# Half a feed-forward piece carried across a step boundary, with Softplus and Erf at later places

## The chip, the cores and the metric

The kernel runs on one core of a Trainium2 chip. The metric is the time of one execution in microseconds (us), as the device measures it. The engines are named as in the profile: PE is the matrix engine, PEld its weight loads, DVE the vector engine, ACT the scalar (activation) engine, POOL the third elementwise engine, and SP the engine that only issues DMAs. A small q behind a name (ACTq, SPq) means the engine's instruction queue, where DMAs are issued.

## The reference

Two blocks follow each other. The first is a linear attention with a decaying state, over 4 sequences of 768 tokens, 8 heads of width 48:

```
for t in range(S):
    cur = einsum('bhd,bhe->bhde', u * kt, vt)
    y[:, :, t] = einsum('bhd,bhde->bhe', rt, state + cur)
    state = wt[..., None] * state + einsum('bhd,bhe->bhde', kt, vt)
```

Its result, as x of 3072 tokens by 384, goes through a feed-forward block with 2048 hidden columns:

```
h = x @ w_in
sp = maximum(h, 0) + log1p(exp(-abs(h)))      # softplus
g = h * erf(sp)
out = g @ w_out
```

All of it is in 32-bit floating point.

## The kernel before

The tokens are cut into 12 steps (`s` from 0 to 11) of 256 tokens: two sequences, 128 tokens each. In step `s`, `attend` (line 350) computes the attention of these tokens. It runs through six levels of masked products (line 390 on PE, into a PSUM tile `pp`), then transposes and state products, and ends with the products at line 498 that finish `y` in PSUM. ACT copies `y` out (lines 505 to 508), and small DMAs issued from SP and ACT (line 512) put the remaining rows into place, so that the tile `xT` holds x, transposed.

The feed-forward of step `s` comes later and is spread in pieces between the attention work of the following steps. It has two generators:

- `hidden` (line 520) makes h = x @ w_in. It works in 8 pieces for a step. A piece is six matmul calls (two column blocks, `ff` 0 and 1, of three accumulating matmuls each), which the trace shows as 12 records at line 547, because each 32-bit matmul stands in it as two. They fill a PSUM tile `m`, which one ACT copy (line 554) moves to the tile `h` in SBUF. Four pieces make one half of the hidden columns. After the last piece of a half, `activate` puts three stages into the list `later`: Softplus (ACT, line 529), Erf (ACT, line 532) and the multiplication (DVE, line 536), each over the whole half.
- `project` (line 559) makes out = g @ w_out.

The PSUM pool of the tiles `m` has two buffers. A third piece can therefore write only when the copy of the one two places before it has been made.

Each step calls `place` eight times: after each of the six levels (places 0 to 5), after the transposes (place 6) and after the state products (place 7). What a place puts into the engines' queues is written out by hand, and each engine takes it in that order. In steps 1 and 2, listed in the table `ALONE`, a place does this, in this order: `convert_at` (the weights are converted there: DVE lines 196 and 199, POOL line 203, then ACT lines 187 and 189 for the next pair of blocks, then a load), `advance(ALONE[s][n])` (takes that many stages from `later`; 0 takes none), and `beside`, which takes one piece of `hidden` of step s - 1:

```
            if s in ALONE:
                convert_at(n)
                advance(ALONE[s][n])
            ...
            beside(s, next(places))
```

So the 8 pieces of step 0's hidden columns lie at the 8 places of step 1, and those of step 1 at the places of step 2. The first piece in step 2 needs `xT` of step 1, which has only just been made at the end of step 1. Where PE would wait for it, `stay_warm` (line 373) puts matmuls of 512 columns whose result nobody reads: one in step 1, two in step 2.

While the weights are converted (to the start of step 3), all the products of `attend` use one of the two `pp` buffers, since the conversion uses the other. The first level's products of step 2 thus need the last reader of the buffer in step 1, the state's update on DVE (line 484), to be done.

Of the kernel before, what the change touches and what calls it, by code (L numbers as in the profile page):

```python
# [22 lines left out]
FG = 8  # L23
FT = 2
# [23 lines left out]
def rights(ap, half):  # L48

    names = "abcdefg"[: len(ap.shape) - 1]  # L50
    spread = " ".join(names)
    return ap.rearrange(f"{spread} (n two h) -> {spread} n two h", two=2, h=half)[
        (slice(None),) * len(names) + (slice(None), 1)
    ]
# [3 lines left out]
def kernel(  # L58
# [25 lines left out]
    NG = NT // FG  # L84
# [37 lines left out]
    def products(shape):  # L122


        n = 0 if turns["converting"] else turns["next"]
        turns["next"] = 1 - n
        return ps_p.tile(shape, FP32, name=f"pp{n}")
# [89 lines left out]
    def rows(e, n=D):  # L217
        return slice(e * EP, e * EP + n)
# [7 lines left out]
    def scale(s, level):  # L226

        in_t, tots = loaded[s][0], ready[s][1]
        half, nb = 1 << (level - 1), JP * C >> level
        halves = view(in_t[:, 0:2], half, [[JP * C - half, 2], [2 * half, nb], [1, half]])  # L230
        nc.vector.tensor_mul(  # L231
            halves, halves, view(tots[level - 1], 0, [[1, 2], [2, nb], [0, half]])
        )
# [116 lines left out]
    def attend(s, xT, place, behind):  # L350
# [14 lines left out]
        def keep_busy(*columns):  # L365
            zeros = states[1][0][:].rearrange("p n d -> p (n d)")
            for n in columns if not s else ():
                nc.tensor.matmul(
                    y[:].rearrange("p e j q t -> p (e j q t)")[:, :n], lhsT=ident[:],
                    rhs=zeros[:, :n], start=True, stop=True, skip_group_check=True,  # L370
                )

        def stay_warm(times=1):
            for _ in range(times):
                ps = ps_m.tile([P, NP * C], FP32, name="m")
                nc.tensor.matmul(
                    ps[:], lhsT=ident[:], rhs=in_t[:, 2, :NP], start=True, stop=True
                )

        for level in range(NEAR_LOG + 1 if s >= DIRECT else 1, LOG + 1):  # L380
            half = 1 << (level - 1)
            rk = made[:] if level == 1 else RK

            pp = products([P, NE, JP, HC])
            m = HC if level <= MASKED else half
            for n in range(JP):
                for s0 in range(0, C, HC):
                    for e in range(NE):
                        t0 = s0 if level <= MASKED else s0 + half
                        nc.tensor.matmul(  # L390
                            pp[s0 : s0 + m, e, n, :m],
                            lhsT=rk[rows(e), 1, n, s0 : s0 + m],
                            rhs=rk[rows(e), 0, n, t0 : t0 + m],
                            start=True,
                            stop=True,
                        )
            keep_busy(DM, DM // 2)
            if level == 1 and s in ALONE:
                stay_warm(s)
            scale(s, level)  # L400
            got = pp[:].rearrange("p e n t -> p (e n) t")
            if level == 1:
                if not s:
                    nc.vector.tensor_copy(out=first[:], in_=mask_sb[:, 0, :])
                nc.vector.tensor_mul(
                    own[:], got, first[:, None, :].to_broadcast([P, NH, HC])
                )
            elif level <= MASKED:
                nc.vector.copy_predicated(  # L409
                    rights(own[:], half),  # L410
                    rights(mask_sb[:, level - 1 : level, :].to_broadcast([P, NH, HC]), half),
                    rights(got, half),
                )
            else:
                for s0 in range(0, C, HC):
                    nc.scalar.copy(  # L416
                        own[s0 : s0 + half, :, half:], got[s0 : s0 + half, :, :half]
                    )
            if level > (NEAR_LOG if s >= DIRECT - 1 else 1):
                next(following, None)  # L420
            place(level - 1)
# [95 lines left out]

    later = []

    def hidden(xT, gs):  # L520


        def activate(h):

            held = []

            def softplus():
                held.append(act.tile([P, FG, UNIT], FP32, name="sp"))
                nc.scalar.activation(held[0][:], h[:], AF.Softplus)  # L529

            def erf():
                nc.scalar.activation(held[0][:], held[0][:], AF.Erf)  # L532

            def multiply():
                for part in (slice(0, FG // 2), slice(FG // 2, FG)):
                    nc.vector.tensor_mul(h[:, part], h[:, part], held[0][:, part])  # L536

            later.extend([(softplus, True), (erf, True), (multiply, False)])

        for g in range(NG):  # L540
            h = hid.tile([P, FG, UNIT], FP32, name="h")
            gs.append(h)
            for f in range(0, FG, FT):
                ps = ps_m.tile([P, FT, UNIT], FP32, name="m")
                for ff in range(FT):
                    for kk in range(KT):
                        nc.tensor.matmul(  # L547
                            ps[:, ff, :],
                            lhsT=w_in_sb[:, g * FG + f + ff, kk * P : (kk + 1) * P],
                            rhs=xT[:, kk, :],  # L550
                            start=kk == 0,
                            stop=kk == KT - 1,
                        )
                nc.scalar.copy(h[:, f : f + FT, :], ps[:])  # L554
                if f == FG - FT:
                    activate(h)
                yield

    def project(s, gs):

        c, i = divmod(s, SPC)
        ps = [None] * NJ
        for g in range(NG):
            for j in range(NJ):
                if not g:
                    ps[j] = ps_m.tile([P, DM], FP32, name="m")
                for f in range(FG):
                    nc.tensor.matmul(  # L568
                        ps[j][:],
                        lhsT=gs[g][:, f, j * C : (j + 1) * C],  # L570
                        rhs=w_out_sb[:, g * FG + f, :],
                        start=g + f == 0,
                        stop=g == NG - 1 and f == FG - 1,
                    )
                    if g == NG - 1 and f == FG - 1:
                        o = outs.tile([P, DM], FP32, name="o")
                        nc.scalar.copy(o[:], ps[j][:])  # L577
                        nc.sync.dma_start(out=out[i * NJ + j, c], in_=o[:])
                    if f % 4 == 3:
                        yield  # L580

    xTs, hids, projs = {}, {}, {}
    gated = [[] for _ in range(n_steps)]

    def advance(count=None):

        while later and count != 0:
            stage, last = later.pop(0)
            stage()
            count = count and count - 1  # L590
            if last and not count:
                break

    def beside(s, k):


        kind, of, pieces = (projs, s - 3, 2) if k < 4 else (hids, s - 1, 2)
        if s >= DIRECT:
            kind, of = (projs, s - 3) if k < 2 else (hids, s - 1)
            pieces = (4, 4, 3, 3, 2)[k]  # L600
        if s in ALONE:
            kind, of, pieces = hids, s - 1, 1
        if not 0 <= of < n_steps:
            return
        if of not in kind:
            kind[of] = hidden(xTs[of], gated[of]) if kind is hids else project(of, gated[of])
        for _ in range(pieces):
            next(kind[of])

# [5 lines left out]
        ("js", "j"),  # L615
    )

    ALONE = {1: (0, 0, 0, 0, 0, 0, 1, 0), 2: (1, 0, 0, 0, 0, 0, 1, 1)}

    make_identity(nc, ident[:])  # L620
    nc.vector.memset(y[:], 0.0)
# [3 lines left out]
    with tc.manual_schedule(  # L625
# [19 lines left out]
        for s in range(n_steps):  # L645
# [3 lines left out]
            def convert_at(n):  # L649
                if s < len(CONVERT) and n < len(CONVERT[s]):  # L650
                    for what in CONVERT[s][n]:
                        conversion.send(what)

            def place(n):
# [3 lines that stand above are left out]
                else:  # L658
                    advance()
                    convert_at(n)  # L660
                beside(s, next(places))
# [6 lines left out]
        for k in range(15):  # L668
            advance()
            beside(n_steps + k // 5, k % 5)  # L670
# [97 lines left out]
```

## Time and profile before

| what | value |
|---|---|
| time, median of 3 runs | 637.16 us (637.15 to 637.78) |
| the profiled run: its time, its span in the profile | 637.19 us, 635.4 us |
| PE busy | 622.5 us (98%), 7338 matmul records |
| ACT busy | 301.3 us (47%), 374 instructions |
| DVE busy | 306.9 us (48%), 311 instructions |
| POOL busy | 276.1 us (43%), 240 instructions |
| step 1's first hidden piece to step 2's first | 36.61 to 73.09 us |
| step 2's first hidden piece to step 3's first projection | 73.09 to 106.73 us |

A row of the timeline gives the start in us from the span's beginning, the duration in us, the engine, the line, the operation with its tiles and their shapes, and how many instructions were merged into the row. In square brackets stand the idle time of that engine just before and what ended it. Neighbouring instructions overlap a little, so the duration of a row may be longer than the distance to the next. In the chain of waits a row gives start, duration and what work the end of the program hung on in that time; "issue" is time in which nothing that the profile shows was waited for.

### The profile page before, as it was taken

The numbers are of one execution on the slowest core, as the hardware profiler recorded it, in microseconds if no ns is written. First come the engines' busy times: TensorE is split into PE (matmuls) and PEld (weight loads), VectorE is DVE, ScalarE is ACT, GpSimd is POOL, SyncE is SP. The second block draws the span as 40 slices with busy tenths as digits, with TensorE's granted clock in tenths as the row PEclk, the third lists the DMA queues.
The fourth block names the chain that finished last, engine by engine and source line by source line (L and its number), as shares of the span: only waits on it lengthen the run. The fifth ranks groups of instructions, "written<-read, shape, count | busy, mean of one in ns | idle before, by whom it ended". The sixth has DMA issues, their size and how long they took to land.

```text
span 635.4 us, 16193 instructions
## 1 busy us (share of the span) xinstructions
PE 622.5 (98%) x7338; PEld 458.2 (72%) x7338; DVE 306.9 (48%) x311; ACT 301.3 (47%) x374; POOL 276.1 (43%) x240
## 2 busy tenths in 40 slices
PE   8889999999999999999999999999999999999997
PEld 7567787678678678668668668768768758768654
DVE  4588597577346256266265365366446322011110
ACT  2537778756424544544534524624624625634520
POOL 4338175495194196097097087088079100000000
PEclk9999999999999999999999999999999999999999
DMA  8366371400500500500510410420330000000000
GB/s 326 130 241 201 136 260 56 200 15 10 206 26 10 207 26 9 206 26 10 183 49 10 168 65 9 152 81 9 103 128 11 8 13 14 7 23 3 1 25 25
DMA packets 24628, 53.84 MB, mean 85 GB/s; under 512 B 11376, under 2 KB 16752, under 8 KB 23152
## 3 DMA queue, kind: packets, MB, share of 16 engines
q1 hardware_dynamic: 23408, 52.23, 23.1%
q8 instruction: 57, 0.93, 0.6%
q10 hardware_dynamic: 1152, 0.59, 0.4%
q14 instruction: 11, 0.09, 0.1%
HBM read 46.39 MB, written 5.24 MB: 81 GB/s over the span
## 4 chain that ended last, share of the span: by engine, by line
PE 91%; DVE 3%; ACT 3%; issue 1%; DMA 1%; POOL 0%; SPq 0%; DVEq 0%; ACTq 0%
PE m L568 40%; PE m L547 38%; PE pp L390 6%; PE y L435 2%; PE pp L446 2%; PE y L498 2%; PE pp L464 2%; DVE in L231 1%; DMA in<-in_rkw 1%; ACT rk L260 1%; DVE own L409 1%; ACT own L416 0%; ACT rest L189 0%; ACT pp L187 0%; DMA xT<-y 0%
## 5 line engine op out<-in xcount | busy, mean ns | idle before, releaser
L547 PE MATMUL m<-xT,w_in_sb 128*128 128x256 f32 x1152 | 260.1, 382 | 0.6 <-DMA xT<-y 0.3
L568 PE MATMUL m<-w_out_sb,h 128*128 128x384 f32 x768 | 253.5, 489 | 0.0
L547 PEld LDWEIGHTS m<-xT,w_in_sb 128*128 128x128 f32 x1152 | 214.6, 190 | 33.2 <-issue 1.6
L568 PEld LDWEIGHTS m<-w_out_sb,h 128*128 128x128 f32 x768 | 144.2, 190 | 97.4
L231 DVE TENSOR_TENSOR in<-in,tot_sb 128x1024 f32<-128x1024 f32 x60 | 80.8, 1347 | 154.4 <-PE pp L390 153.2
L536 DVE TENSOR_TENSOR h<-h,sp 128x1024 f32<-128x1024 f32 x48 | 80.3, 1713 | 67.7 <-ACT sp L532 67.7
L554 ACT COPY h<-m 128x512 f32<-128x512 f32 x96 | 56.2, 586 | 104.2 <-PE m L547 104.0
L577 ACT COPY o<-m 128x384 f32<-128x384 f32 x24 | 11.5, 479 | 148.4 <-PE m L568 136.6
L289 POOL TENSOR_TENSOR rk<-words,u_row 128x768 f32<-128x768 f32 x8 | 17.3, 2157 | 124.8 <-DMA words<-in_rk_rows 124.8
L306 POOL TENSOR_TENSOR tot_sb<-tot_sb 128x256 f32<-128x256 f32 (+4 forms) x60 | 54.1, 902 | 4.5
L390 PEld LDWEIGHTS pp<-in 48*64 48x64 f32 (+1 forms) x2816 | 41.0, 127 | 20.5 <-issue 17.5
L295 POOL TENSOR_TENSOR words<-words,rest 128x576 f32<-128x576 f32 (+5 forms) x48 | 52.6, 1096 | 3.8
L390 PE MATMUL pp<-in 48*64 48x64 f32 (+1 forms) x2816 | 46.5, 214 | 4.2 <-DVE own L409 2.3
L532 ACT ACTIVATE sp<-sp 128x2048 f32<-128x2048 f32 x24 | 45.9, 1911 | 0.3
L529 ACT ACTIVATE sp<-h 128x2048 f32<-128x2048 f32 x24 | 45.9, 1911 | 0.3
L532 ACT ACT_TABLE_LOAD x24 | 30.8, 1283 | 20.4 <-issue 20.2
L296 POOL TENSOR_TENSOR words<-words 128x480 f32<-128x480 f32 (+4 forms) x40 | 32.8, 819 | 3.1
L529 ACT ACT_TABLE_LOAD x24 | 30.8, 1283 | 3.0 <-issue 2.6
L296 POOL TENSOR_TENSOR rk<-words 128x672 f32<-128x672 f32 (+1 forms) x16 | 31.9, 1994 | 0.6
L324 DVE TENSOR_REDUCE sums<-words 128x10 f32<-128x480 f32 (+4 forms) x40 | 17.7, 452 | 26.5 <-POOL words L296 25.9
L203 POOL TENSOR_TENSOR w_out_sb<-w_out_sb,rest 128x768 int32<-128x768 int32 x8 | 18.1, 2271 | 27.4 <-DVE w_out_sb L199 27.4
L476 DVE TENSOR_TENSOR middle<-faded,pp 48x384 f32<-48x384 f32 x20 | 11.0, 552 | 32.9 <-PE pp L464 32.6
(57 smaller groups left out, 427.2 us busy)
## 6 DMA issues: line engine op xcount, KB each, us to landing
in<-in_rkw SPq DMA_DIRECT2D x11, 1536.0 KB, 6.6
words<-in_moe_w_in SPq DMA_DIRECT2D x8, 768.0 KB, 6.0
words<-in_moe_w_out SPq DMA_DIRECT2D x8, 768.0 KB, 4.8
words<-in_rk_rows SPq DMA_DIRECT2D x8, 768.0 KB, 8.4
v<-in_v SPq DMA_DIRECT2D x12, 384.0 KB, 7.0
out<-o SPq DMA_DIRECT2D x24, 192.0 KB, 1.9
rest<-in_w_rows SPq DMA_DIRECT2D x8, 384.0 KB, 8.9
in<-in_rkw SPq DMA_DIRECT2D x2, 512.0 KB, 4.6
```

The costliest lines, as they stand in the source:

```text
L203: nc.gpsimd.tensor_tensor(out=into, in0=into, in1=rest[:], op=ALU.add)
L231: nc.vector.tensor_mul(halves, halves, view(tots[level - 1], 0, [[1, 2], [2, nb], [0, half]]))
L295: nc.gpsimd.tensor_mul(k[:, : NEAR - n], k[:, : NEAR - n], w[:, n - 1 : NEAR - 1])
L296: nc.gpsimd.tensor_mul(terms[n], r[:, n:], k[:, : NEAR - n])
L306: nc.gpsimd.tensor_mul(new, pair[:, :, 0], pair[:, :, 1])
L390: nc.tensor.matmul(pp[s0 : s0 + m, e, n, :m], lhsT=rk[rows(e), 1, n, s0 : s0 + m], rhs=rk[rows(e), 0, n, t0 : t0 + m], start=True, stop=True,)
L529: nc.scalar.activation(held[0][:], h[:], AF.Softplus)
L532: nc.scalar.activation(held[0][:], held[0][:], AF.Erf)
L536: nc.vector.tensor_mul(h[:, part], h[:, part], held[0][:, part])
L547: nc.tensor.matmul(ps[:, ff, :], lhsT=w_in_sb[:, g * FG + f + ff, kk * P : (kk + 1) * P], rhs=xT[:, kk, :], start=kk == 0, stop=kk == KT - 1,)
L554: nc.scalar.copy(h[:, f : f + FT, :], ps[:])
L568: nc.tensor.matmul(ps[j][:], lhsT=gs[g][:, f, j * C : (j + 1) * C], rhs=w_out_sb[:, g * FG + f, :], start=g + f == 0, stop=g == NG - 1 and ...
```

## The change

`hidden` is told by `cut` whether it is step 0's. If it is, the last of its eight pieces stops once more after its first column block, that is in the middle of the piece. The eighth place of step 1 then does only this first half. The first place of step 2 takes the second half, before the first piece of step 1's hidden columns; the ACT copy of the whole piece comes with the second half, and so does the entry of the second half's stages into `later`.

The two `stay_warm` matmuls at the first level of step 2 are gone; step 1 keeps its one.

`ALONE` changes as well. Softplus of step 0's first half, which stood at place 6 of step 1, is now at place 0 of step 2. Its Erf, which stood at place 0 of step 2, is now at place 2. Its multiplication stays at place 6 of step 2, and Softplus of the second half at place 7.

```diff
@@ attend
-            if level == 1 and s in ALONE:
-                stay_warm(s)
+            if level == 1 and s == 1:
+                stay_warm()
@@ hidden
-    def hidden(xT, gs):
+    def hidden(xT, gs, cut):
...
                             start=kk == 0,
                             stop=kk == KT - 1,
                         )
+                    if cut and not ff and g == NG - 1 and f == FG - FT:
+                        yield
                 nc.scalar.copy(h[:, f : f + FT, :], ps[:])
@@ beside
         if s in ALONE:
             kind, of, pieces = hids, s - 1, 1
+            if s == 2 and not k:
+
+                next(hids[0])
...
-            kind[of] = hidden(xTs[of], gated[of]) if kind is hids else project(of, gated[of])
+            kind[of] = hidden(xTs[of], gated[of], not of) if kind is hids else project(of, gated[of])
@@
-    ALONE = {1: (0, 0, 0, 0, 0, 0, 1, 0), 2: (1, 0, 0, 0, 0, 0, 1, 1)}
+    ALONE = {1: (0,) * 8, 2: (1, 0, 1, 0, 0, 0, 1, 1)}
```

## The prediction, made before the changed kernel was run

> **What bounds the kernel now.** I read the page first. Its busy line and the head of its chain say where a change can count at all.
>
> ```profile
> PE 622.5 (98%) x7338; PEld 458.2 (72%) x7338; DVE 306.9 (48%) x311; ACT 301.3 (47%) x374; POOL 276.1 (43%) x240
> PE 91%; DVE 3%; ACT 3%; issue 1%; DMA 1%; POOL 0%; SPq 0%; DVEq 0%; ACTq 0%
> ```
>
> PE is the bound. The list of PE's waits from 107 us to the end is empty, so whatever PE loses or gains before 107 us is carried to the end whole. The question is only what happens between the end of step 1 and the start of step 3. For that I took PE's timeline (from the eighth piece of step 0's hidden columns on), and then ACT's for the same stretch.
>
> ```profile
> 66.48 2.86 PE L547 MATMUL m<-xT,w_in_sb 128*128 128x256 f32 x12
> 69.27 0.66 PE L498 MATMUL y<-in,middle 48*48 48x64 f32 x32
> 69.76 1.11 PE L390 MATMUL pp<-rk 48*64 48x64 f32 x64
> 70.80 1.99 PE L376 MATMUL m<-in,ident 128*128 128x512 f32 x4
> 73.09 3.25 PE L547 MATMUL m<-xT,w_in_sb 128*128 128x256 f32 x12 [0.30 <-DMA xT<-y]
> 76.27 1.16 PE L390 MATMUL pp<-in 48*64 48x64 f32 x64
> 77.36 2.86 PE L547 MATMUL m<-xT,w_in_sb 128*128 128x256 f32 x12
> 80.38 1.16 PE L390 MATMUL pp<-in 48*64 48x64 f32 x64 [0.16 <-DVE own L409]
> ```
>
> From y's end (about 69.95) to the arrival of x at 73.09 PE has 1.04 us of needed products, 1.99 of `stay_warm` and 0.30 idle. So there is about 2.1 us to fill. I call the pieces of step 2 q0 (73.09), q1 (77.36), q2 and so on, and the moved piece p8 (66.48).
>
> ```profile
> 65.46 1.28 ACT L529 ACT_TABLE_LOAD   x1
> 66.76 1.91 ACT L529 ACTIVATE sp<-h 128x2048 f32<-128x2048 f32 x1
> 68.58 0.57 ACT L554 COPY h<-m 128x512 f32<-128x512 f32 x1
> 69.38 0.59 ACT L554 COPY h<-m 128x512 f32<-128x512 f32 x1 [0.24 <-PE m L547]
> ...
> 75.99 0.88 ACT L187 ACTIVATE pp<-words 128x768 f32<-128x768 f32 x1 [1.20 <-DVE w_out_sb L199]
> 76.81 0.91 ACT L189 ACTIVATE rest<-words 128x768 int32<-128x768 uint32 x1
> 77.73 1.28 ACT L532 ACT_TABLE_LOAD   x1
> 79.03 1.91 ACT L532 ACTIVATE sp<-sp 128x2048 f32<-128x2048 f32 x1
> 80.84 0.57 ACT L554 COPY h<-m 128x512 f32<-128x512 f32 x1
> ```
>
> The last row is what I rest on most. It is q0's copy; q0's matmuls ended at 76.34, yet the copy starts at 80.84, because Erf stands before it in ACT's queue. It ends at 81.41, and q2, which needs the buffer, starts at 81.47. It costs PE almost nothing today only because q1's buffer is free: the last user of it was a `stay_warm` matmul, which nobody reads.
>
> **What the Trainium skill says.** "PSUM — Partial Sum Buffer", section "Engine vs sequencer instructions": the queues of ScalarE, VectorE and GpSimdE are strict first in, first out. The trace agrees, by the 4.5 us of that copy. "ScalarE: Activation LUTs", section "What ACT_TABLE_LOAD costs": 1283 ns for the load, and with a drain 2.66 us for a switch. The trace has the 1283, but the function begins 1.30 us after its load, so I use 3.11 us for Erf or Softplus with its load (77.73 to 80.84). "TensorE: Matmul & The Clock Gate", section "What's actually happening": an idle window of about 3.4 us may put PE at half clock until it has been busy as long. PE's longest wait in this trace is 1.7 us, so no run shows it yet; that PE starts slow it does show (the warm-up matmuls of line 630, 128 columns, median 421 ns, fastest 275).
>
> **The change part by part.** First what gains. The first half of p8 is 6 of 12 records, half of 2.79 us, so 1.40. It ends at 66.55 + 1.40 = 67.95. The y products also need `middle`, which DVE ends at 67.31, so they run at once, end at 68.59 instead of 69.98, and everything down to the landing of x comes 1.39 us earlier: first rows at 71.70. PE meanwhile wants level 1's products. Their buffer is read by the state update on DVE (line 484), which ends at 69.38 and doesn't move. So PE idles 0.8 us, does the products from 69.42 to 70.46, and p8's second half to 71.86. The first rows of x are there. q0 has its later rows no sooner than 1.39 us earlier than now, so it ends at 76.34 - 1.39 = 74.95. This is the whole gain: 1.39 us. The 1.99 us of `stay_warm` that are gone are not counted again, since they stood in the same wait.
>
> Softplus of the first half leaves place 6 of step 1 (3.2 us of ACT). Nobody waited for it: the y copies start at 70.00, as soon as y is there. So nothing is gained. No DMA, no SP and no POOL instruction is among what moves; the weight loads on SP and the joins on POOL keep their order and are only pulled or pushed along with ACT's conversion. The number of table loads stays.
>
> Now what is queued behind it. At place 0 of step 2 ACT gets, in order: the two conversion instructions, Softplus (instead of Erf), **the copy of p8**, the copy of q0. And q1 at place 1 needs a PSUM buffer out of two: one holds p8, the other q0, and both copies stand behind Softplus. The conversion pair starts when DVE has joined the one before, which follows from the y copies: 75.99 - 1.39 = 74.60. Softplus' load then starts at 77.73 - 1.39 = 76.34, the copy of p8 at + 3.11 = 79.45, and ends at 80.02. q1 starts at about 80.06. It would have been ready at 74.95 + 1.09 (level 2's products) = 76.0. So PE waits some 4.0 us. Against before (77.40) q1 is 2.66 late. Level 3's products, which waited 0.16 for DVE (that is over by then), follow at 82.85 instead of 80.38: 2.47 late.
>
> Then Erf at place 2. It stands behind the conversion pair there and before q2's copy. Before, that pair began 5.35 us after level 3's products (80.38 to 85.73, DVE's chain of four instructions between). DVE is half a microsecond less behind then, so I take 4.85: 87.70. The pair takes 1.65, Erf 3.11, q2's copy 0.57: 93.03. q4 needs that buffer. PE gets to it at 82.85 + 3 x 1.09 + 2 x 2.79 = 91.70, so it waits 1.35. ACT is now the chain itself: next level multiplications for step 3 (1.76), a pair (1.63), q3's copy; q5 waits another 0.35 for that one. The next pair can't begin before DVE has joined the one before, at 94.68 + 0.86 + 0.04 + 0.97 + 0.95 = 97.5; then 1.65 for the pair, 0.47 for q4's copy and 1.17 for the two copies of level 6 (line 416): 100.83. These PE waits for: its second group of `own` products, at 96.46 before, starts at 100.87. That is **4.4 us late**: -1.39 from the half piece, +4.05 behind Softplus, -0.2 for the small wait that goes, +1.9 behind Erf.
>
> After that the places are as before. Multiplication, second Softplus and state products stand where they stood, DVE and ACT have room in step 3 (ACT waits 4.47 us for its first output copy there), and PE doesn't wait again. Span 635.4 + 4.4 = 639.8. The profiled run took 637.19 us, 0.03 above the median, so the time is 641.6.
>
> **The bounds of what the trace doesn't show.** Whether PE's clock drops in a wait of 4 us: nothing at the low end; at the high end up to 3.4 us of work at half speed, an estimate from the skill's window, 1.7 us lost, and a little more if the window falls badly: 2.5. I take nothing, since the wait is barely longer than the window and the window isn't started by it. The gain can't pass 1.7 (it would need the x rows not to bind q0). ACT's chain with Erf: if PE's levels push ACT less than I reckoned, 0.8 less; if pairs and copies lie worse, 0.8 more.
>
> **The rivals.** First, the half piece fills the wait and nothing else happens: 1.39 us faster, 635.8. The place is q1's start. It decides if p8's copy is over by 76.0, that is if ACT does Softplus before about 72.3 or the copy before Softplus. For it: ACT has gaps (1.20 and 1.91 us) there, and the change takes work out of step 1's end. Against it: `place` calls `advance` before `beside`, and the trace shows exactly that order in the 80.84 row. The turning point is a wait of 1.4 us at q1. Second, the wait of 4 us also halves PE's clock: 4.4 + 1.9 = 6.3 slower, 643.5. For it the length of the wait; against it the phase. Third, only the first wait costs, and Erf at place 2 finds room because PE and DVE have run behind anyway: 2.5 slower, 639.7. Against it: from 87.7 to 100.8 I find no gap of ACT but 0.6 us.
>
> **How the numbers follow.** My forecast has 0.68, the clock rival 0.16, the first wait alone 0.08, together 0.92 slower. The gain alone has 0.06; 0.02 remain for the two cancelling. A measurement of this kernel can tell about 0.2%, or 1.3 us, from no change; all the slower cases are beyond it, and the gain just about. The forecast's own range is 640.7 to 642.5. With the third case below and the clock above, the range is 639.6 to 644.2.
>
> **What would show it.** In the changed profile: y's products end near 68.6, and q0 begins near 71.9. PE has one wait of about 4 us before q1, ended by an ACT copy at line 554 near 80.0, which directly follows Softplus (line 529). q4 waits again, 1 to 2 us, for the copy behind Erf. Step 3's first projection starts near 111.1 instead of 106.73. Matmuls of q1 above 400 ns would show the clock. I am wrong if q1 starts before 77.4, or if PE gets back what it lost after 107 us.

## The result and the profile after

The changed kernel takes 644.24 us (643.88 to 645.16, 4 runs) against 637.17 of the kernel before: a ratio of 1.0111, 95% interval 1.0093 to 1.0128. It is 7.1 us slower; 4.4 were forecast. The profiled run is the longest of the four, with a span of 643.4 us; it had PE at half clock from 11.3 to 18.2 us too, ahead of anything that was changed, and it is 0.39 us behind by the first moved instruction. In what follows such differences are counted from that instruction on.

The page's busy line and the head of its chain first.

```profile
PE 624.4 (97%) x7334; PEld 459.8 (71%) x7334; DVE 313.6 (49%) x311; ACT 301.3 (47%) x374; POOL 277.3 (43%) x240
PE 89%; ACT 3%; DMA 3%; DVE 2%; issue 1%; POOL 1%; ACTq 0%; SPq 0%
```

PE has four records fewer than before and is still busy 1.9 us longer: some of its work has become slower. PE's timeline says which.

```profile
66.87 1.56 PE L547 MATMUL m<-xT,w_in_sb 128*128 128x256 f32 x6
68.36 0.67 PE L498 MATMUL y<-in,middle 48*48 48x64 f32 x32
69.91 1.16 PE L390 MATMUL pp<-rk 48*64 48x64 f32 x64 [0.89 <-DVE s L484]
71.01 4.51 PE L547 MATMUL m<-xT,w_in_sb 128*128 128x256 f32 x18
75.44 1.16 PE L390 MATMUL pp<-in 48*64 48x64 f32 x64
80.64 5.49 PE L547 MATMUL m<-xT,w_in_sb 128*128 128x256 f32 x12 [4.03 <-ACT h L556]
86.05 1.31 PE L390 MATMUL pp<-in 48*64 48x64 f32 x64
...
94.95 1.16 PE L390 MATMUL pp<-in 48*64 48x64 f32 x64 [0.92 <-DVE own L409]
96.62 2.86 PE L547 MATMUL m<-xT,w_in_sb 128*128 128x256 f32 x12 [0.51 <-ACT h L556]
99.41 0.76 PE L390 MATMUL pp<-in 48*32 48x32 f32 x64
100.48 2.86 PE L547 MATMUL m<-xT,w_in_sb 128*128 128x256 f32 x12 [0.32 <-ACT h L556]
```

The half piece is there (6 records at 66.87) and its other half runs straight into q0 (18 records at 71.01): the wait for x is gone. Then q1 stands at 80.64 behind a wait of 4.03 us for an ACT copy, and takes 5.49 us where it took 2.86. Smaller waits come before level 5, q4 and q5. ACT's timeline shows what the long wait was for (the copy, line 554 before, is line 556 here):

```profile
75.17 0.88 ACT L187 ACTIVATE pp<-words 128x768 f32<-128x768 f32 x1 [1.21 <-DVE w_out_sb L199]
75.99 0.90 ACT L189 ACTIVATE rest<-words 128x768 int32<-128x768 uint32 x1
76.90 1.28 ACT L529 ACT_TABLE_LOAD   x1
78.20 1.91 ACT L529 ACTIVATE sp<-h 128x2048 f32<-128x2048 f32 x1
80.01 1.06 ACT L556 COPY h<-m 128x512 f32<-128x512 f32 x2
```

The two copies, of p8 and of q0, are one row right behind Softplus. The clock that PE was granted comes next, in short stretches of that time. A row has the stretch, its length, the busy time of PE, PEld, DVE, ACT and POOL (in brackets how many instructions), and then the mean granted clock (1.00 is full), the DMA engines' share and their GB/s:

```profile
79.00:79.40 0.40, 0.00 (x0) 0.00 (x0) 0.40 (x2) 0.40 (x1) 0.00 (x0) 1.00 0.85 330
79.40:79.80 0.40, 0.00 (x0) 0.00 (x0) 0.40 (x2) 0.40 (x1) 0.00 (x0) 0.75 0.85 338
86.20:86.40 0.20, 0.20 (x12) 0.20 (x16) 0.00 (x0) 0.20 (x1) 0.00 (x0) 0.50 0.00 0
86.40:86.60 0.20, 0.20 (x24) 0.20 (x20) 0.00 (x0) 0.20 (x1) 0.00 (x0) 0.94 0.00 0
```

From 79.40 to 79.80 the mean is 0.75, that is half of the stretch at full clock and half at half clock. So the clock fell to half at about 79.6, 3.0 us after the last matmul, and came back at 86.4, just after q1. The places at which PE fell behind, against the kernel before:

| up to | behind, us | step, us |
|---|---|---|
| end of q0 | -1.22 | -1.22, the half piece |
| start of q1 | 2.89 | +4.11, the copy behind Softplus |
| start of q2 | 5.43 | +2.54, half clock, less the 0.16 wait that went |
| first projection of step 3 | 7.58 | +2.15, the waits before level 5, q4, q5 and line 435 |

### The profile page after: what moved, and what is told of

Same layout as the page of the kernel before. It is cut to its first block, busy times and chain, and to the rows that moved or that the text cites. A ratio compares the mean times of both kernels' runs of the same rounds, so it can differ in the third digit from the quotient of the medians.

```text
span 643.4 us, 16184 instructions
## 1 busy us (share of the span) xinstructions
PE 624.4 (97%) x7334; PEld 459.8 (71%) x7334; DVE 313.6 (49%) x311; ACT 301.3 (47%) x374; POOL 277.3 (43%) x240
## 4 chain that ended last, share of the span: by engine, by line
PE 89%; ACT 3%; DMA 3%; DVE 2%; issue 1%; POOL 1%; ACTq 0%; SPq 0%
PE m L570 39%; PE m L547 36%; PE pp L390 6%; DMA in<-in_rkw 3%; PE y L435 2%; PE pp L446 2%; PE y L498 2%; PE pp L464 2%; ACT pp L187 1%; DVE pp L196 1%; POOL tot_sb L306 1%; ACT rest L189 0%; DVE in L231 0%; DVE w_out_sb L199 0%; DVE own L409 0%
## 5 line engine op out<-in xcount | busy, mean ns | idle before, releaser
L231 DVE TENSOR_TENSOR in<-in,tot_sb 128x1024 f32<-128x1024 f32 x60 | 88.8, 1480 | 158.0 <-PE pp L390 156.1
L289 POOL TENSOR_TENSOR rk<-words,u_row 128x768 f32<-128x768 f32 x8 | 15.9, 1993 | 122.0 <-DMA words<-in_rk_rows 122.0
L390 PEld LDWEIGHTS pp<-in 48*64 48x64 f32 (+1 forms) x2816 | 42.4, 131 | 20.4 <-issue 16.8
L296 POOL TENSOR_TENSOR words<-words 128x480 f32<-128x480 f32 (+4 forms) x40 | 35.3, 883 | 3.1
```

The lines of the kernel that those rows point to most:

```text
L231: nc.vector.tensor_mul(halves, halves, view(tots[level - 1], 0, [[1, 2], [2, nb], [0, half]]))
L296: nc.gpsimd.tensor_mul(terms[n], r[:, n:], k[:, : NEAR - n])
L390: nc.tensor.matmul(pp[s0 : s0 + m, e, n, :m], lhsT=rk[rows(e), 1, n, s0 : s0 + m], rhs=rk[rows(e), 0, n, t0 : t0 + m], start=True, stop=True,)
```

## The experiments

The kernel before, on the same chip, stands beside each, and the ratio is to it. I call "behind by the profile" the distance from p8's start to step 3's first projection, less the 40.25 us of before; the changed kernel has 7.58 there.

**The half piece alone.** Softplus and Erf go back to their places.

```diff
-    ALONE = {1: (0,) * 8, 2: (1, 0, 1, 0, 0, 0, 1, 1)}
+    ALONE = {1: (0, 0, 0, 0, 0, 0, 1, 0), 2: (1, 0, 0, 0, 0, 0, 1, 1)}
```

> The changed kernel with Softplus and Erf at their places of before: only the half piece is moved and the two unread matmuls are gone. Theory (the copy of the straddling piece stands behind whatever function ACT has at place 0, and PE's long wait costs it its clock): Erf stands there as Softplus did, so PE waits about 4 us before the second piece of step 2 and then runs it at half clock. The y copies begin about 0.6 us later than in the changed kernel, since Softplus is again before them. Sum against before: +3.2 by the wait, +2.7 by the clock, -0.2: about 643. Rival (the moved functions are the cause, the half piece is harmless): about 636, faster than before.

Measured: 643.83 us, 1.0105 (1.009 to 1.012), behind by 7.19. PE waits 4.06 us before q1 and q1 takes 5.49. The half piece does nearly all of it, whichever function stands at place 0; the rival is out. The expectation missed one thing: 1.35 us of the 7.19 come after q2 has started, and 0.92 of them are a wait for DVE, though Erf is at its old place here:

```profile
95.09 1.16 PE L390 MATMUL pp<-in 48*64 48x64 f32 x64 [0.92 <-DVE own L409]
```

The changed kernel has the same wait. It can thus arise without Erf at place 2; a later experiment looks at it.

**Softplus and Erf alone**, in the kernel before.

```diff
-    ALONE = {1: (0, 0, 0, 0, 0, 0, 1, 0), 2: (1, 0, 0, 0, 0, 0, 1, 1)}
+    ALONE = {1: (0,) * 8, 2: (1, 0, 1, 0, 0, 0, 1, 1)}
```

> The kernel before with only the table of places changed: Softplus at place 0 and Erf at place 2 of step 2, no half piece, both unread matmuls kept. Theory: Softplus at place 0 does what Erf did there, nothing; Erf at place 2 holds back the copy of the third piece, so that the fifth waits about 1.9 us, which ACT carries to the end of the step: about 639.1, no loss of clock. Rival (the moved functions make the loss of 7 us): 642 or more. Second rival (Erf finds room): 637.2.

Measured: 639.75 us, 1.0042 (1.0027 to 1.0057), behind by 2.56. PE's timeline of this kernel has the wait at q4:

```profile
87.71 1.16 PE L390 MATMUL pp<-in 48*64 48x64 f32 x64
90.79 2.86 PE L547 MATMUL m<-xT,w_in_sb 128*128 128x256 f32 x12 [1.91 <-ACT h L554]
```

The wait of 1.91 us is as expected, and after it the piece runs in 2.86. So the two moved functions cost 2.6 us alone, and the long wait is the one behind Erf at place 2. In the changed kernel less of that was left, 7.58 with it against 7.19 with the half piece alone. From q2's start on the difference is 0.80 (2.15 against 1.35), since part of the wait behind Erf falls into the time of the wait for DVE before level 5.

**PE kept busy in the wait.** Four unread matmuls into y's buffer before q1.

```diff
             keep_busy(DM, DM // 2)
+            for _ in range(4 if s == 2 and level == 2 else 0):
+                nc.tensor.matmul(
+                    y[:].rearrange("p e j q t -> p (e j q t)")[:, : NP * C], lhsT=ident[:],
+                    rhs=in_t[:, 2, :NP], start=True, stop=True, skip_group_check=True,
+                )
```

> The changed kernel with four unread matmuls of 512 columns (about 1 us each) after the products of level 2 in step 2, written into y's buffer, so that PE works through the wait. Theory of the clock: the second piece still starts when the copy is done, but takes 2.8 us instead of 5.5: about 641.5, and the granted clock in that stretch is full. Rival (the loss beyond 4.4 us is not the clock but DVE and the conversions behind it): still about 644.

Measured: 642.19 us, 1.0081 (1.0066 to 1.0096), behind by 4.80.

```profile
76.12 3.70 PE L399 MATMUL y<-in,ident 128*128 128x512 f32 x8
80.22 2.86 PE L552 MATMUL m<-xT,w_in_sb 128*128 128x256 f32 x12 [0.40 <-ACT h L561]
```

Useless work added makes it no slower than the changed kernel, rather faster (4.80 behind against 7.58, and against 6.47 in the repeated run of the changed kernel below; the intervals of the ratios overlap a little). q1 begins as late as there but takes 2.86 us. So the clock is the cause of q1's length, and without it the rest of the change costs 4.8 by the profile: what I had forecast as 4.4.

**The same with one unread matmul** (`range(1 ...)`), to see how long PE must be silent.

> The changed kernel with one unread matmul (about 1 us) after the products of level 2 in step 2, so that PE's wait ahead of the second piece is 3.1 us and not 4. If the clock falls only after 3.4 us of silence: the piece runs in 2.8 us, about 642.2 as with four of them. If about 3 us from the last matmul are enough, the clock falls as the piece begins and it is slow, if for less long: 643.5 to 644.

Measured: 644.67 us, 1.012 (1.0106 to 1.0135), behind by 6.43. The wait is 2.98 us, the clock falls at 80.66, just before q1 at 80.77, and q1 takes 4.47. One matmul isn't enough. The median lies above both expectations; in the profiled execution the clock fell at 36.3 us too, ahead of anything that was changed.

**The copy ahead of Softplus**, still behind the conversion pair.

```diff
                     convert_at(n)
+                    if s == 2 and not n:
+                        next(hids[0])
                     advance(ALONE[s][n])
...
-            if s == 2 and not k:
-
-                next(hids[0])
```

> The changed kernel with the second half of the straddling piece, and with it its copy, ahead of Softplus in the first place of step 2 (still behind the conversion pair). Theory of the queue: the copy is made at about 77.5 instead of 80.6, the second piece waits about 1 us instead of 4, the clock holds, and what is left is Erf at place 2: about 639. If the buffer of the straddling piece is not what the second piece waits for: still about 644.

Measured: 641.32 us, 1.0061 (1.0044 to 1.0077), behind by 4.03. q1 now waits 0.80 us, ended by the same copy: the buffer of p8 is what it waited for. But 639 was wrong, since q4 loses its clock in turn. PE's timeline, and the clock after it:

```profile
92.14 4.54 PE L547 MATMUL m<-xT,w_in_sb 128*128 128x256 f32 x12 [2.20 <-ACT h L556]
```

```profile
91.50:92.00 0.50, 0.00 (x0) 0.00 (x0) 0.50 (x2) 0.50 (x3) 0.50 (x2) 1.00 0.39 98
92.00:93.00 1.00, 0.86 (x3) 0.73 (x4) 0.13 (x1) 1.00 (x5) 1.00 (x1) 0.88 0.95 369
93.00:94.00 1.00, 1.00 (x4) 0.81 (x3) 0.00 (x0) 1.00 (x4) 1.00 (x2) 0.50 0.74 309
```

A wait of 2.20 us was enough here, where 1.91 wasn't in the run with the stages alone. The mean of 0.88 from 92 to 93 us is full clock to about 92.76 and half from there: the clock fell when q4 was already running.

**The two unread matmuls of step 2 taken out** of the kernel before.

```diff
-                stay_warm(s)
+                stay_warm(s if s == 1 else 0)
```

> The kernel before without the two unread matmuls of step 2, nothing else. PE then has a wait of about 2.2 us for x. If they only stood in the wait: 637.0. If a wait of 2.2 us is enough for the clock, as in the run with the copy first: the first piece runs slow, about 638.5.

Measured: 638.1 us over 22 runs, 1.0011 (1.0005 to 1.0018): about 0.7 us slower. PE waits 2.21 us for x. In the profiled execution the clock stays full there and q0 takes 3.26, as before. Between the two expectations, then. One stretch of 3.4 us at half clock takes about 0.003 off the mean clock of an execution (worked out from the span of 635.7 us), so a mean of 0.995 or less is more than one such stretch. Of these runs 8 of 22 had that, against 6 of 45 of the kernel before beside it. That fits a wait that costs the clock in some executions only, but no profile here caught one.

**Is the wait for DVE before level 5 a part of it?** In the changed kernel the level 4 multiplication on DVE (line 231) takes 2.87 us, 1.22 or 1.23 at the levels beside it, and begins 0.04 us after POOL's join (line 203). A small POOL copy now holds that join back.

```diff
+    seen = const.tile([P, 64], I32, name="seen")
...
+                if i == 10:
+                    nc.gpsimd.tensor_copy(out=seen[:], in_=into[:, 0, :64])
                 nc.gpsimd.tensor_tensor(out=into, in0=into, in1=rest[:], op=ALU.add)
```

> The changed kernel with one small copy of 64 columns on POOL ahead of the join of the weights (line 203) at place 2 of step 2, so that DVE's multiplication for level 4 (line 231) begins before that join and not 0.04 us after it. Theory (where the two overlap, the one that starts later stands until the other is done): the multiplication takes about 1.3 us instead of 2.87, the join about 2.7 instead of 1.82, PE's wait of 0.92 us for DVE before level 5 goes: up to 0.9 us less than the changed kernel, less if the copies behind Erf take up part of it. Rival (DVE is slow there for another reason): no change.

The changed kernel again, on the same chip:

> The changed kernel as it is, on the same chip as the run with the small copy on POOL: 1.011 of the kernel before, the wait of 4 us and half clock behind it.

Measured: 643.92 us with the small copy, 1.0095 (1.008 to 1.011), and 643.72 without, 1.0092 (1.0075 to 1.0109). The rows of the timeline for DVE's multiplication and POOL's join, first with the small copy and then without:

```profile
90.09 1.23 DVE L234 TENSOR_TENSOR in<-in,tot_sb 128x1024 f32<-128x1024 f32 x1 [0.19 <-PE pp L393]
...
90.28 2.71 POOL L206 TENSOR_TENSOR w_out_sb<-w_out_sb,rest 128x768 int32<-128x768 int32 x1
```

```profile
89.96 1.82 POOL L203 TENSOR_TENSOR w_out_sb<-w_out_sb,rest 128x768 int32<-128x768 int32 x1 [6.97 <-DVE w_out_sb L199]
...
90.01 2.85 DVE L231 TENSOR_TENSOR in<-in,tot_sb 128x1024 f32<-128x1024 f32 x1 [0.19 <-PE pp L390]
```

The one that starts later stands until the other is done: 2.85 us for DVE's instruction where it starts 0.05 us after POOL's, and 2.71 instead of 1.82 for POOL's where it starts 0.19 us after DVE's. The Trainium skill says so in "SBUF — State Buffer", section "SBUF: two separate sides", of a DVE instruction with two inputs in SBUF against a POOL instruction that reads SBUF, as these two are: whichever comes first holds the port pair that they share for its whole duration, and the other is blocked. PE's wait of 0.92 before level 5 is gone, and yet nothing is gained: q4, the next piece, now waits 1.52 for its copy instead of 0.50. Here the wait for DVE stood in the same time as the wait behind Erf, and with the one gone the other shows. From q2's start to step 3's first projection 2.16 us are lost with the small copy and 2.13 without. In the half piece alone, where Erf is not behind it, the small copy might gain; that was not run. In the repeated run of the changed kernel q1 took 4.54 us, not 5.49, and PE was 6.47 behind by the profile: how long the clock stays low differs from one execution to the next.

**Both pieces first.** At the first place of step 2, p8's second half and q0, with their copies, come ahead of the conversion and of the function; Softplus and Erf are at their places of before.

```diff
+                if s == 2 and not n:
+                    beside(s, next(places))
+                    convert_at(n)
+                    advance(ALONE[s][n])
+                    return
                 if s in ALONE:
...
-    ALONE = {1: (0,) * 8, 2: (1, 0, 1, 0, 0, 0, 1, 1)}
+    ALONE = {1: (0, 0, 0, 0, 0, 0, 1, 0), 2: (1, 0, 0, 0, 0, 0, 1, 1)}
```

> The half piece moved as in the changed kernel, Softplus and Erf at their places of before, and at the first place of step 2 both pieces (with their copies) ahead of the conversion and of Erf. Theory of the queue: no piece waits for a copy behind Erf, the gain of the half piece comes through, less about 0.4 us because Softplus is again ahead of the y copies: about 636.2. Rival (the later conversion costs as much on DVE and ACT): 637 or more.

Measured over 21 runs: 636.46 us against 637.47, 0.9985 (0.9979 to 0.9992), 0.99 ahead by the profile. Its PE timeline:

```profile
71.06 4.76 PE L547 MATMUL m<-xT,w_in_sb 128*128 128x256 f32 x18
75.75 1.16 PE L390 MATMUL pp<-in 48*64 48x64 f32 x64
76.84 2.86 PE L547 MATMUL m<-xT,w_in_sb 128*128 128x256 f32 x12
79.86 1.16 PE L390 MATMUL pp<-in 48*64 48x64 f32 x64 [0.15 <-DVE own L409]
```

q1 follows level 2 without a wait. The half piece's gain is real, and this order beats both kernels.

**The same order with the changed kernel's places** of Softplus and Erf.

> The changed kernel with both pieces, and their copies, ahead of the conversion and of Softplus at the first place of step 2; Softplus and Erf as in the changed kernel. Theory: the gain of 1.2 us from the half piece, then the loss behind Erf at place 2 that the stages alone showed (2.4 us), and perhaps half clock after a wait of 2 us as in the run with the copy first (1.7 us): 638.2, with the clock 639.9. Rival (the moved Erf costs only together with the wait for the copy): 636.

Measured: 639.32 us, 1.0027 (1.0016 to 1.0038), behind by 1.35. q4 waits 1.92 us behind Erf again and keeps its clock in the profiled execution. Erf at place 2 thus loses more than the half piece gains, even when no copy stands in the way of q1.

## Why the prediction was wrong

The direction, the wait behind Softplus and the wait behind Erf were right. One term of the sum, which I had put at nothing, was 2.7 us in the profiled run.

- **The gain.** Forecast 1.39, measured 1.22 (1.23 in the repeated run). The wait for DVE's state update before level 1 came as worked out (0.89 against 0.8), and q0's later rows of x set its end.
- **Softplus leaving step 1 gains nothing.** Nothing by itself (with the two functions moved alone, q0 starts 6.60 us after p8, against 6.61 before), but it is needed for the whole gain: with Softplus back ahead of the y copies q0 ended 0.24 us later (the half piece alone, 8.81 after p8's start against 8.57).
- **The copy behind Softplus.** Forecast a wait of 4.0 us, measured 4.03; q1 forecast at 80.06, measured at 80.64, less 0.39 of the early offset. The run with the copy ahead of Softplus shows it is this copy.
- **The failed step: PE's clock.** I wrote "I take nothing, since the wait is barely longer than the window and the window isn't started by it." It cost 2.7 us in the profiled run (the 2.54 of the table and the 0.16 that went) and 1.6 in the repeated one. I took the Trainium skill's window of about 3.4 us ("TensorE: Matmul & The Clock Gate", section "What's actually happening") as what a wait has to exceed. A wait of 2.20 was enough in one run and one of 2.98 in another, and all five waits of 2.98 us or more that were profiled lost the clock, so the phase that I counted on against it did not help. The rival that had the clock (6.3 slower, chance 0.16) was the right case. It was short in that it valued the loss at 1.9, and by the 0.4 below.
- **Erf at place 2.** Forecast 1.9 for what follows q2, measured 2.15. The wait I put at q4 (1.35) showed up as 0.92 before level 5 and 0.51 at q4, 1.43 together. The first part has a cause that the forecast did not see, DVE's multiplication standing behind POOL's join. It did not add to the sum, since without it the wait behind Erf takes its place, as the run with the small POOL copy shows. The rival that Erf at place 2 finds room is out by the run of the two functions alone (2.56 behind). The rest is 0.32 at q5, as against the 0.35 I had, and ACT's longer way to line 435.
- **After 107 us** nothing was given back, as forecast.

With PE kept busy the change costs 4.8 by the profile: the forecast without the clock, and 0.4.

## What to carry to other kernels

Before work is moved across a boundary, ask who reads its buffer and what stands in that reader's queue at the new place: here an idle wait of 2 us was filled well, and a copy behind a 3 us function then held the only two buffers. Put copies that free buffers ahead of long functions. And price a new wait on PE with the clock it may lose: where the clock fell at a wait of 2.2 to 4.1 us, the piece behind it took 1.5 to 2.6 us longer. Unread matmuls in such a wait may be worth keeping.

## What the runs showed of the hardware

In six profiles PE's clock fell to half in or just behind one of the waits above, worked out from the mean clock of short stretches as above: at 2.8 us (the copy first), 2.9 (one unread matmul), 3.0 (the changed kernel), 3.4 (the half piece alone), 3.7 (the small POOL copy) and 4.1 (the changed kernel again) after the last matmul, in the first of these 0.6 us after PE had begun again. It stayed there for 3.4 us in four of them and for 6.8 in two, once and twice the window of about 3.4 us of which the Trainium skill speaks ("TensorE: Matmul & The Clock Gate", section "What's actually happening"); that makes the difference between 4.54 and 5.49 us for q1. In the profiled executions waits of 1.91 and 1.92 us left the clock alone, so did one of 2.21, and one of 2.20 did not. The two with 1.91 and 1.92 are the fastest of their kernels, and others of these took up to 1.5 us longer; whether such a wait cost them the clock is not shown.

A fall can also follow shorter waits. Five more lie ahead of everything that was moved: at 11.3 us (the changed kernel), 17.3 (the unread matmuls taken out), 24.5 (both pieces first), 36.3 (one unread matmul) and 36.1 (the changed kernel again). In the 3.4 us before them no single wait of PE was longer than 0.94, 1.78, 0.91, 1.32 and 1.32 us. The last of them, PE's row and then the clock:

```profile
34.70 1.16 PE L390 MATMUL pp<-rk 48*64 48x64 f32 x64 [1.32 <-DVE s L484]
```

```profile
36.00:37.00 1.00, 1.00 (x2) 0.38 (x2) 1.00 (x2) 0.29 (x1) 0.31 (x1) 0.55 0.17 42
```

The kernel before has a wait of 1.32 us there too, ahead of its row at 34.56, and kept its full clock in its profile; of 45 other executions of it 19 had a mean clock of 0.997 or less. So the length of a wait alone doesn't decide. The skill's section says of the window that it runs freely, which fits this scatter. But neither a wait of 2.20 us nor one of 1.32 fills a window, so by these profiles it doesn't take a wholly idle one. How much idleness it takes isn't settled.
